# Other durations in a planner's model: scans, DMA packets and operations off partition 0, with all offsets derived anew

## The chip, the core and the metric

The kernel runs on one core of a Trainium2 chip. The metric is the device time of one execution in microseconds (us). The time shown for a kernel is the median of its runs; beside it stands one profiled execution with a time of its own, from which all durations below are read. The core's engines are PE (matmuls; PEld are its weight loads), DVE (vector), ACT (scalar), POOL and SP, which here issues nearly all DMAs. Each engine runs its instructions in the order in which they stand in its queue and waits at the first one that is not ready.

## The reference

Three parts in a row, for 4 batches, 8 heads, 768 steps, head size 40:

```python
for t in range(S):                      # attention: a recurrence over a 40x40 state per head
    y[:, :, t] = einsum('bhd,bhde->bhe', rt, state)
    Sa = einsum('bhde,bhe->bhd', state, at)
    state = state * wt - einsum('bhd,bhe->bhde', Sa, bt) + einsum('bhd,bhe->bhde', vt, kt)
x = y as [3072, 320]
h = x @ w_in;  x = (h * cos(h)) @ w_out                          # first MoE, 320 -> 2048 -> 320
h = x @ w_in2; out = (h * clip(h + 3, 0, 6) / 6) @ w_out2        # second MoE
```

## The kernel before, in words

The recurrence is cut into 12 chunks of 64 steps. Work is done per chunk c and batch b (unit n = 4c + b). Values are kept as pairs of fp16 numbers (a high and a low part), so a product is several matmuls.

Per unit, `pA`, `pB`, `pT`, `pC` load the inputs (raw), multiply them by decays (pip), make fp16 pairs (KBs, ARs), transpose them by DMA (KBT, ART) and form the triangular matrix (LN, NT), which `pL` stores. Per chunk, for all batches and heads at once, the inverse of that matrix is made: `iL` loads the triangles (Lt<-Ls), `iB` runs 31 steps on DVE, each a product into tmp and an addition into Tt, `iC` copies the result (four copies S8a<-Tt among them) and `iC1` sends it through DRAM (Tm<-Tt, Tm<-S8a, Thl<-Tt, then Lt<-Tm and TT<-Thl). `iD` and `iE` multiply 32x32 blocks on PE (tile q), and each of the two `iE` of a chunk ends with a DVE operation TT<-q,TT. Then come the units' recurrence steps `cV`, `cU`, `cA`, `cAT`, `cG`, `cF` (tiles FS, uh, GF, xy, S8a, ST), and `cXT` transposes a unit's output by DMA into x1T, the input of the first MoE.

`mA(m, c, j)` is a group of 16 matmuls of MoE m (into tile h), an ACT function (s<-h), a DVE product (s) and the fp16 pair ghl; `mB` multiplies ghl by wout (tile acc). m = 0 reads x1T, m = 1 reads x2T. Chunk c's `mA` can begin when the four units of chunk c have their x1T.

At the start the decays are computed by scans (`decay`, tensor_tensor_scan over 650 elements, 24 of them), and the weights are loaded and converted in passing (`ld_w`, `prep_w`).

The order of all this is made by the class `Plan` while the program is built. Every operation is recorded with a duration (`rec`). `order` plays the engines forward with these durations: at each moment an engine takes, of the operations that are ready, the one with the best priority. A priority is the length of the work that hangs on an operation, plus offsets in the table `TUNE`, one entry for each kind of step (an offset for all, two for the first two chunks, a release time, and one for each operation of the step). `AHEAD` and `MARGIN` say when an engine stays idle for a better operation that is about to be ready. Some operations may go to either of two engines: casts and copies to DVE or ACT, elementwise ones to DVE or POOL; the plan takes whichever comes free. `emit` (lines 415 and 419) then writes the instructions in that order, so nearly every instruction in the trace has line 419 (or 415, for a copy on ACT) and is told by its tiles.

Of the kernel before, what the change touches and what calls it, by code (L numbers as in the profile page):

```python
# [45 lines left out]


TUNE = {
    "decay_const": (406, -4, -216, 2, (69, -5)),
    "decay0": (0, 509, 274, 0, (1, 42, -5, -44, -13, -34, -127, -64, -11, 116, -48, -99, 17, -40, -43, 12, -192,  # L50
        -141, -67, -15, -3, 6, -4, 32, -39, -1, -6, -10, 7, 22, -66, -28, -2, -6, 10, -7, -48)),
    "consts": (97, -153, -168, 11, (-19, 91, 1, -32, -33, 38, 4, -23, 79, 145, -9, 10, -75, 14, 4, 6, 11, -12, -35)),
    "consts1": (-254, 100, 347, 0, (-14,)),
    "consts2": (60, 417, 197, 0, (-11, -4, -48)),
    "pA": (0, 51, -99, 0, (-1, 41)),
    "pB": (0, -16, -1, 39, (0, 0, -1, 0, 0, 0, 1)),
    "pT": (-1, 70, -30, 0, (2,)),
    "pC": (-20, -1, -45, 0, (0, 2, -8, 14)),
    "pL": (1, 5, 467, 0, (-1,)),
    "rest": (124, -153, -38, 17, (-10, -2)),  # L60
    "dsq0": (-68, 293, -36, 0, (18,)),
    "chunk_decay": (-5, 51, -56, 118, (-27, 37, 3, 51)),
# [11 lines left out]
    "cAT": (-74, 88, -241, 0, (-60,)),  # L74
    "cD": (-18, 7, -10, 82, (-13,)),
    "cG": (-2, -8, 9, 21, (-28, 0, -11, -7, 20, -2)),
    "cF": (-13, 1, 0, 173, (-19, 0, 0, 6, 4, 4, 6, 0, 0, -3)),
    "cXT": (-45, -151, 140, 0, (1,)),
    "cST": (5, -4, -19, 35, (2, 2, -5, -2)),
# [19 lines left out]
    "wcol": (-50, 302, -353, 190, (-20, -7, 0, -170, 60, -60, 105)),  # L99
    "flags": (153, -38, 4, 0, (-83, -72, 51, 21, 31, -14, 76, 60, 30, -72, 81, -15, -68, -54, -25, 111, -3, -24,  # L100
        -19, 131, -91, -99, 96, -71, 64, -111)),
}
HALVES = ((0, 0), (1, 0))
SHARE = 20
SLACK, AHEAD, MARGIN = [132, 0, 20, 0, 383], [0, 150, 70, 54], [422, 48, 296, 22]
RING = {"raw": 2560, "KBT": 2048, "LN": 2048, "v": 1280, "uh": 640, "FT": 2048, "gm": 2048, "pd": 2560, "xy": 1280,
        "wst": 2048, "wx": 1024, "s": 2048, "xs2": 1536, "ghl": 2048, "E": 1280, "ART": 2048, "NT": 1152}

# [25 lines left out]
T_SHAPE = 96.0  # L134
FULL = (128, 128)
POOL_GAIN = 0.25
LAT = {"PE": 190, "DVE": 125, "ACT": 140, "POOL": 70}


class Plan:  # L140
# [9 lines left out]
    def cover(self, ap):  # L150
        t = ap.tensor
        es = mybir.dt.size(ap.dtype)
        dims = [(a, b) for a, b in ap.ap if b > 1 and a]
        off = ap.offset
        dram = t._space == DRAM
        u = 32 if dram else 2
        key = (off, tuple(dims), es)
        m = self.masks.get((t.name, key))
        if m is not None:
            return m  # L160
        p0, p1 = 0, 1
        if not dram:
            row = 1
            for k in t.shape[1:]:
                row *= k
            p0, off = divmod(off, row)
            p1 = p0 + ap.ap[0][1]
            dims = [(a, b) for a, b in list(ap.ap)[1:] if b > 1 and a]
        off += sum(a * (b - 1) for a, b in dims if a < 0)
        dims = sorted((abs(a), b) for a, b in dims)  # L170
        run = 1
        while dims and dims[0][0] <= run:
            run += dims[0][0] * (dims[0][1] - 1)
            dims.pop(0)
        lo, hi = off * es // u, -(-(off + run) * es // u)
        if not dram:
            hi += sum(a * (b - 1) for a, b in dims) * es // u
            dims = []
        m = (1 << (hi - lo)) - 1
        for a, b in dims:  # L180
            sh, k = a * es // u, 1
            while 2 * k <= b:
                m |= m << sh * k
                k *= 2
            m |= m << sh * (b - k)
        m = (p0, p1, m << lo)
        self.masks[t.name, key] = m
        return m
# [20 lines left out]
    def rec(self, attr, eng, name, a, kw):  # L209
        i = len(self.ops)  # L210
# [9 lines left out]
        if name.startswith("dma"):  # L220
            sb = outs[0] if outs[0].tensor.__class__.__name__ == "Tile" and outs[0].tensor._space != DRAM else ins[0]
            c = 475.0 if sb.shape[0] in (32, 128) or ins[0].ap[0][0] == 0 else 650.0
            by = 1
            for k in outs[0].shape:
                by *= k
            by *= mybir.dt.size(outs[0].dtype)
            if name == "dma_start":
                run = _run(outs[0], ins[0])
                dma = by / 360.0 * (2 if run < 512 else 1)
            else:  # L230
                r, w = ins[0].shape[0], by // 2 // ins[0].shape[0]
                dma = w / 128 * 112 * r / 128
                c = 1244.0 if r == 128 and w >= 1024 else 1175.0
        elif eng == "PE":
            c = max(n / 2.4 + 2.5, 28.0)
            shape = tuple(32 if x <= 32 else 64 if x <= 64 else 128 for x in (ins[0].shape[0], _free(ins[0])))
        elif eng in ("DVE", "ANY"):
            c = 70 + n * 1.042
            es = max(mybir.dt.size(x.dtype) for x in outs + ins)
            if name == "tensor_copy":  # L240
                c = 70 + n * (0.26 if es == 2 else 0.52)
            elif name == "tensor_scalar":
                c = 70 + n * 0.52
            elif name == "reciprocal":
                c = 70 + n * 6.3
            if any(_free(x) == 1 for x in ins):
                c += 60
        elif eng == "ACT":
            c = 95 + n * 0.833
            if "accum_out" in kw:  # L250
                c += 93
            elif "bias" in kw:
                c += 50
            elif ins[0].tensor._space == PSUM:
                c -= 42
# [11 lines left out]
            o["shape"] = shape  # L267
        else:
            o = dict(eng=eng, c=c, alt=cp if eng in ALTS else None, dma=dma, deps=set(), prio=self.prio, calls=[],
                     grp=(self.group, outs[0].tensor.name), i=i, port=False, shape=FULL)  # L270
            self.ops.append(o)
            if eng == "PE" and shape != FULL:
                o["c"] += 2 * T_SHAPE
                o["shape"] = shape

            o["port"] = name not in ("memset", "tensor_reduce", "reciprocal") and all(getattr(x.tensor, "_space", None) != PSUM for x in ins)
        o["calls"].append((attr, name, a, kw))
        for x in ins:
# [4 lines left out]
    def order(self):  # L283
# [36 lines left out]
        soon = [set() for _ in engs]  # L320
        evs = []
        start = [0] * n
        gone = set()
        dmaf = dge = end = 0

# [36 lines left out]
        while evs:  # L362
# [14 lines left out]
            for e in sorted(touched):  # L377
# [7 lines left out]
                if e < 4 and AHEAD[e] > 0:  # L385
                    lim = 100 * t + c * AHEAD[e]
                    if any(100 * ready_t[u] < lim and pr[u] < pr[i] - 400 * MARGIN[e] for u in soon[e]):
                        continue
                gone.add(i)
                o["on"] = engs[e]  # L390
                start[i] = t
# [57 lines left out]
def _free(ap):  # L449
    n = 1  # L450
    for k in ap.shape[1:]:
        n *= k
    return n


def _run(o, i):
# [1012 lines left out]
```

## Time and profile before

| | us |
|---|---|
| median of 3 runs | 1272.9 |
| lowest, highest | 1268.25, 1284.62 |
| the profiled execution, its own time | 1271.3 |
| its span in the profile | 1269.4 |
| mean granted TensorE clock of the profiled execution | 0.935 of 2.4 GHz |

The span is from the first to the last instruction; 1.9 us of the execution's time lie around it. Rows of the trace name an engine, a line, an operation, its tiles as out<-in with partitions x elements, and times in us from the span's start. PEclk is the granted clock: 1.00 is 2.4 GHz, 0.50 is 1.2 GHz. "Idle before" is the time that an engine stood still ahead of an instruction, with the engine or DMA that ended it.

### The profile page before, as it was taken

The numbers are of one execution on the slowest core, as the hardware profiler recorded it, in microseconds if no ns is written. First come the engines' busy times: TensorE is split into PE (matmuls) and PEld (weight loads), VectorE is DVE, ScalarE is ACT, GpSimd is POOL, SyncE is SP. The second block draws the span as 40 slices with busy tenths as digits, with TensorE's granted clock in tenths as the row PEclk, the third lists the DMA queues.
The fourth block names the chain that finished last, engine by engine and source line by source line (L and its number), as shares of the span: only waits on it lengthen the run. The fifth ranks groups of instructions, "written<-read, shape, count | busy, mean of one in ns | idle before, by whom it ended". The sixth has DMA issues, their size and how long they took to land.

```text
span 1269.4 us, 29683 instructions
## 1 busy us (share of the span) xinstructions
PE 910.1 (72%) x11378; PEld 732.8 (58%) x11378; DVE 1067.0 (84%) x2434; ACT 792.8 (62%) x1642; POOL 180.4 (14%) x206
## 2 busy tenths in 40 slices
PE   0010033571668889699899898988999899999995
PEld 0000023561457668577777676766777777778874
DVE  8999999889989988869989799698796997967543
ACT  1664358485678667657676577686766866645352
POOL 2322111123423110101000010010120100100000
PEclk9999999795679899789999899899898999999998
DMA  6997478775787584776767748868477674532010
GB/s 204 244 186 177 107 225 151 159 162 124 149 171 148 108 156 102 134 144 103 130 143 135 142 83 151 148 113 155 103 126 150 115 134 93 94 63 46 11 24 14
DMA packets 474362, 162.65 MB, mean 128 GB/s; under 512 B 446789, under 2 KB 456049, under 8 KB 473826
## 3 DMA queue, kind: packets, MB, share of 16 engines
q1 hardware_dynamic: 473922, 160.00, 62.6%
q8 instruction: 91, 1.49, 0.5%
q10 hardware_dynamic: 288, 0.67, 0.2%
q14 instruction: 61, 0.50, 0.1%
HBM read 80.10 MB, written 25.61 MB: 83 GB/s over the span
## 4 chain that ended last, share of the span: by engine, by line
DVE 42%; PE 23%; DMA 11%; ACT 8%; issue 6%; SPq 3%; POOL 0%; DVEq 0%; ACTq 0%; POOLq 0%
PE acc L419 9%; PE h L419 8%; DVE Tt L419 6%; DVE tmp L419 5%; DVE S8a L419 4%; DVE ghl L419 4%; DVE wout L419 4%; PE q L419 4%; DVE s L419 3%; SPq L419 3%; DMA Lt<-Tm 2%; DVE win L419 2%; PE t L419 2%; DVE FS L419 2%; DVE GF L419 2%
## 5 line engine op out<-in xcount | busy, mean ns | idle before, releaser
L419 PE MATMUL acc<-wout,ghl 128*128 128x320 f16 x2304 | 371.8, 309 | 36.7 <-DVE ghl L419 29.6
L419 PEld LDWEIGHTS <-win 128*128 128x128 f16 x3328 | 312.1, 101 | 74.3 <-issue 27.6
L419 PEld LDWEIGHTS <-ghl 128*128 128x128 f16 x2304 | 217.1, 100 | 122.2 <-DVE ghl L419 35.1
L419 PE MATMUL h<-x1T,win 128*128 128x256 f16 (+1 forms) x1664 | 192.9, 275 | 25.4 <-DVE s L419 17.5
L419 ACT ACTIVATE s<-h,cvec 128x512 f32<-128x512 f32 x192 | 130.4, 680 | 119.4 <-PE h L419 81.8
L419 PE MATMUL h<-x2T,win 128*128 128x256 f16 (+1 forms) x1664 | 187.0, 267 | 0.0
L419 DVE TENSOR_TENSOR ghl<-s,ghl 128x512 f16<-128x512 f32 x182 | 127.6, 703 | 8.7 <-ACT ghl L415 5.2
L419 PE MATMUL p<-ART,KBT 120*128 120x64 f16 x384 | 21.4, 204 | 124.1 <-DMA ART<-ARs 73.7
L419 DVE TENSOR_TENSOR tmp<-Tt,Lt 128x126 f32<-128x126 f32 (+22 forms) x372 | 104.9, 282 | 6.5 <-DMA Lt<-Ls 3.3
L419 DVE TENSOR_TENSOR Tt<-Tt,tmp 128x126 f32<-128x126 f32 (+22 forms) x372 | 103.6, 279 | 3.6
L415 ACT ACTIVATE ghl<-s 128x512 f16<-128x512 f32 x127 | 79.3, 625 | 34.7 <-DVE s L419 27.3
L419 DVE SCALAR_TENSOR_TENSOR s<-h,s 128x512 f32<-128x512 f32 x96 | 65.7, 686 | 38.0 <-ACT s L419 37.5
L419 DVE SCALAR_TENSOR_TENSOR s<-s,h 128x512 f32<-128x512 f32 x96 | 65.2, 680 | 33.6 <-ACT s L419 33.2
L419 PEld LDWEIGHTS <-KBT 120*128 120x128 f16 x384 | 18.7, 104 | 127.7 <-DMA KBT<-KBs 84.7
L419 PE MATMUL t<-E,GF 128*128 128x40 f16 x1152 | 46.1, 184 | 40.1 <-DVE GF L419 32.3
L419 PE MATMUL q<-Lt,Tt 32*32 32x32 f32 x768 | 32.9, 203 | 49.3 <-DMA Lt<-Tm 49.3
L419 PEld LDWEIGHTS <-GF 128*128 128x128 f16 x1152 | 38.7, 99 | 49.1 <-DVE GF L419 34.5
L419 POOL TENSOR_TENSOR wout<-wout 128x512 int32<-128x512 int32 (+1 forms) x28 | 50.2, 1802 | 103.4 <-ACT wout L419 73.2
L419 PEld LDWEIGHTS q<-Lt,Tt 32*32 32x32 f32 x768 | 30.1, 118 | 53.5 <-issue 35.9
L419 PE MATMUL t<-FS,NT 128*128 128x40 f16 x768 | 36.7, 183 | 22.2 <-DVE FS L419 12.4
L419 POOL TENSOR_TENSOR S8a<-S8a,pd 40x320 f32<-40x320 f32 x23 | 25.7, 1123 | 176.0 <-DMA pd<-Ds 175.6
L419 PEld LDWEIGHTS <-ART 120*64 120x64 f16 (+1 forms) x704 | 43.9, 106 | 6.7 <-issue 4.4
(157 smaller groups left out, 1764.1 us busy)
## 6 DMA issues: line engine op xcount, KB each, us to landing
raw<-in_arbk_dram SPq DMA_DIRECT2D x46, 320.0 KB
v<-in_vv_dram SPq DMA_DIRECT2D x96, 80.0 KB
pip<-Dec SPq DMA_DIRECT2D x46, 160.0 KB
wout<-in_moe_w_in_dram SPq DMA_DIRECT2D x12, 512.0 KB
Ls<-LN SPq DMA_DIRECT2D x48, 128.0 KB
Lt<-Ls SPq DMA_DIRECT2D x48, 128.0 KB
TT<-Thl SPq DMA_DIRECT2D x12, 512.0 KB
wstat<-in_moe_w_out_dram SPq DMA_DIRECT2D x10, 512.0 KB
```

The lines of the kernel that those rows point to most:

```text
L415: self.nc.scalar.activation(func=AF.Copy, **kw)
L419: getattr(getattr(self.nc, attr), name)(*a, **kw)
```

## The change

Four durations in the planner's model change. A scan is booked at 70 + 2.08 n ns instead of 70 + 1.042 n. A DMA is booked by its packets, 9 ns and 0.045 ns a byte each over 16 engines, instead of 360 GB/s with a doubling under 512 bytes; a DMA transpose at 204 instead of 112 ns for 128 columns. An operation of DVE or ACT whose output or input starts off partition 0 takes 110 ns more, and so does the one behind it. The key under which the planner keeps an access also has its number of partitions. With that model all numbers of `TUNE`, `AHEAD` and `MARGIN` are derived anew.

```diff
 TUNE = {
-    "iL": (2, 22, -1287, 19, (-27, 0, -88, 35)),
+    "iL": (4, -6, -1396, 19, (-1, -36, -88, 10)),
...
-SLACK, AHEAD, MARGIN = [132, 0, 20, 0, 383], [0, 150, 70, 54], [422, 48, 296, 22]
+SLACK, AHEAD, MARGIN = [132, 0, 20, 0, 383], [0, 164, 69, 10], [319, 48, 324, 54]
...
+OFFSET = 110
...
-        key = (off, tuple(dims), es)
+        key = (off, tuple(dims), es, ap.ap[0][1])
...
                 run = _run(outs[0], ins[0])
-                dma = by / 360.0 * (2 if run < 512 else 1)
+                run = min(run, 20480)
+                dma = by / run * (9 + run * 0.045) / 16
             else:
                 r, w = ins[0].shape[0], by // 2 // ins[0].shape[0]
-                dma = w / 128 * 112 * r / 128
+                dma = w / 128 * 204 * r / 128
...
+            elif name == "tensor_tensor_scan":
+                c = 70 + n * 2.08
...
+            o["off"] = OFFSET if any(_part(x) for x in outs[:1] + ins) else 0
...
+        was = [0] * 5
...
+                if e in (1, 2):
+                    c, was[e] = c + max(o["off"], was[e]), o["off"]
...
+def _part(ap):
+
+    row = 1
+    for k in getattr(ap.tensor, "shape", ())[1:]:
+        row *= k
+    return ap.offset >= row
```

(Engine 1 is DVE, engine 2 is ACT.) What the program computes stays as it is, and each engine has as many instructions as before but for a few that change engines; their order is another nearly everywhere. Two places show it.

The first is DVE's queue in chunk 7, from the middle of the work behind the last inverse step up to the first TT<-q,TT. Before, 19 instructions stand between that step and this TT; these are the last of them:

```order
L419 SCALAR_TENSOR_TENSOR s_147<-h_145,s_147 128x512
L419 TENSOR_TENSOR ghl_150<-s_148,ghl_150 128x512
L419 TENSOR_TENSOR S8a<-S8a,pd_142 40x320
L419 TENSOR_TENSOR ghl_151<-s_147,ghl_151 128x512
L419 SCALAR_TENSOR_TENSOR s_148<-h_146,s_148 128x512
L419 CAST ghl_149<-s_148 128x512
L419 TENSOR_TENSOR ghl_149<-s_148,ghl_149 128x512
L419 SCALAR_TENSOR_TENSOR s_147<-h_145,s_147 128x512
L419 TENSOR_TENSOR LN_135<-p_134,mskL 128x512
L419 CAST NT_115<-LN_135 64x512
L419 TENSOR_TENSOR ghl_150<-s_147,ghl_150 128x512
L419 SCALAR_TENSOR_TENSOR TT<-q_137,TT 32x16x32
```

In the new order 26 instructions stand between the two, and these are the last:

```order
L428 TENSOR_TENSOR ghl_149<-s_148,ghl_149 128x512
L428 TENSOR_TENSOR NT_114<-LN_135,NT_114 64x512
L428 SCALAR_TENSOR_TENSOR s_147<-h_145,s_147 128x512
L428 CAST ghl_150<-s_147 128x512
L428 TENSOR_TENSOR ghl_150<-s_147,ghl_150 128x512
L428 SCALAR_TENSOR_TENSOR s_148<-h_146,s_148 128x512
L428 CAST ghl_151<-s_148 128x512
L428 TENSOR_TENSOR ghl_151<-s_148,ghl_151 128x512
L428 TENSOR_TENSOR raw_116<-raw_116,pip_80 128x640
L428 CAST KBs_76<-raw_116 128x8x2x40
L428 SCALAR_TENSOR_TENSOR TT<-q_137,TT 32x16x32
```

One more MoE group (s, ghl) and a unit's raw and KBs operations, which stood behind the TT, now stand ahead of it.

The second is SP's queue in the same chunk, from the first store of the inverse to the load that brings it back (Lt<-Tm). Before:

```order
L419 DMA Tm_106<-Tt 64x16x32
L419 DMA Tm_106<-S8a 64x16x32
L419 DMA Thl_108<-Tt 64x16x32 x4
L419 DMA_TRANSPOSE KBT_125<-KBs_77 128x8x128
L419 DMA Lt_92<-Tm_106 64x1024
L419 DMA Ls_103<-LN_135 64x16x32
```

After:

```order
L428 DMA Tm_106<-Tt 64x16x32
L428 DMA Srep_89<-Tt 40x16x40
L428 DMA Thl_108<-Tt 64x16x32
L428 DMA Tm_106<-S8a 64x16x32
L428 DMA Thl_108<-Tt 64x16x32 x3
L428 DMA_TRANSPOSE ART_129<-ARs_79 128x8x128
L428 DMA Ls_103<-LN_135 64x16x32
L428 DMA Lt_92<-Tm_106 64x1024
```

The load keeps its place behind the stores; a store of LN, an ART transpose and one of the three Srep copies have come in front of it, and a KBT transpose has gone elsewhere.

## Rows read from the trace of the kernel before

**Rows 1.** The page, busy us (share of the span) and instructions of each engine.

```profile
PE 910.1 (72%) x11378; PEld 732.8 (58%) x11378; DVE 1067.0 (84%) x2434; ACT 792.8 (62%) x1642; POOL 180.4 (14%) x206
```

**Rows 2.** The chain that ended last, share of the span by engine.

```profile
DVE 42%; PE 23%; DMA 11%; ACT 8%; issue 6%; SPq 3%; POOL 0%; DVEq 0%; ACTq 0%; POOLq 0%
```

**Rows 3.** Busy time by stage: stretch, its length, each engine's busy us, granted clock.

```profile
core 0: us, PE busy (x) PEld busy (x) DVE busy (x) ACT busy (x) POOL busy (x), PEclk, DMA share, GB/s
...
534.00:1163.00 629.00, 576.21 (x7242) 462.28 (x7239) 531.84 (x1294) 425.86 (x921) 53.99 (x77) 0.96 0.65 120
1163.00:1247.00 84.00, 84.00 (x726) 67.00 (x724) 41.86 (x86) 34.92 (x72) 0.00 (x0) 1.00 0.10 19
```

**Rows 4.** The same table for the round trips: chunk 7, and the sum over ten.

```profile
786.90:813.10 26.20, 22.22 (x261) 16.84 (x261) 15.28 (x26) 14.79 (x30) 2.25 (x6) 0.87 0.91 145
...
sum 261.50, PE 227.33 PEld 178.16 DVE 171.65 ACT 152.25 POOL 24.74; mean PE 22.73 PEld 17.82 DVE 17.16 ACT 15.22 POOL 2.47
```

**Rows 5.** The same table for the nine stretches between the round trips, summed.

```profile
sum 515.30, PE 460.85 PEld 372.65 DVE 494.59 ACT 382.17 POOL 62.06; mean PE 51.21 PEld 41.41 DVE 54.95 ACT 42.46 POOL 6.90
```

**Rows 6.** The chain of work within 785 to 815 us: start, us, what.

```profile
795.73 3.75 DMA Lt<-Tm
799.52 1.19 PE q L419 x32
...
802.11 1.84 PE q L419 x32
...
804.86 3.41 PE h L419 x16
...
812.99 1.76 PE h L419 x16
```

**Rows 7.** DVE's timeline there; in brackets the idle time before and its end.

```profile
804.61 0.69 DVE L419 SCALAR_TENSOR_TENSOR TT<-q,TT 32x512 f16<-32x512 f32 x1 [1.65 <-ACT TT L419]
...
809.03 0.69 DVE L419 SCALAR_TENSOR_TENSOR s<-h,s 128x512 f32<-128x512 f32 x1 [3.02 <-ACT s L419]
```

**Rows 8.** The table by stretch, for the clock in chunks 7 and 3.

```profile
795.00:801.50 6.50, 4.65 (x68) 3.79 (x67) 3.26 (x6) 1.41 (x3) 0.00 (x0) 1.00 1.04 200
801.50:808.30 6.80, 6.80 (x57) 4.60 (x56) 2.77 (x5) 1.55 (x3) 0.00 (x0) 0.50 0.90 131
...
521.00:528.30 7.30, 2.73 (x63) 2.24 (x62) 6.42 (x18) 4.47 (x10) 1.47 (x1) 0.73 0.54 117
```

**Rows 9.** Groups by form: count, busy us, mean ns of one, idle before.

```profile
L419 DVE TENSOR_TENSOR_SCAN win<-win 128x650 f32<-128x650 f32 x24 | 38.2, 1607 | 3.7 <-DMA win<-in_wfwd_dram 3.3 <-ACT win L419 0.3
...
L419 DVE CAST ghl<-s 128x512 f16<-128x512 f32 x65 | 28.4, 437 | 10.0 <-PE acc L419 8.0
```

**Rows 10.** DVE's timeline at 608 to 611 us: start, us, instruction.

```profile
608.14 0.69 DVE L419 TENSOR_TENSOR LN<-p,mskL 128x512 f32<-128x512 f32 x1
608.74 0.27 DVE L419 TENSOR_TENSOR tmp<-Tt,Lt 128x120 f32<-128x120 f32 x1
...
609.82 0.69 DVE L419 TENSOR_TENSOR NT<-LN,NT 64x512 f16<-64x512 f32 x1
610.53 0.29 DVE L419 TENSOR_TENSOR tmp<-Tt,Lt 128x121 f32<-128x121 f32 x1
```

**Rows 11.** PE's timeline at the end of chunks 3 and 10.

```profile
522.13 0.57 PE L419 MATMUL t<-E,GF 128*128 128x40 f16 x16
...
1094.70 5.05 PE L419 MATMUL acc<-wout,ghl 128*128 128x320 f16 x36
```

**Rows 12.** The chain of work within 522 to 529 us.

```profile
525.77 2.47 DMA x1T<-S8a
```

**Rows 13.** PE's waits, 534 to 1131 us: us in total, times, longest.

```profile
PE q L419 <- DMA Lt<-Tm: 12.2, 7, 2.6
...
PE h L419 <- DMA x1T<-S8a: 3.3, 4, 1.1
```

More of the change, by code (lines that the diff above doesn't have):

```diff
@@ L48 @@
 TUNE = {
[L49 to L62, printed above, removed]
[11 rows of a table removed]
[L74 to L77, printed above, removed]
@@ L78 @@
-    "cXT": (-45, -151, 140, 0, (1,)),
-    "cST": (5, -4, -19, 35, (2, 2, -5, -2)),
[19 rows of a table removed]
-    "wcol": (-50, 302, -353, 190, (-20, -7, 0, -170, 60, -60, 105)),
-    "flags": (153, -38, 4, 0, (-83, -72, 51, 21, 31, -14, 76, 60, 30, -72, 81, -15, -68, -54, -25, 111, -3, -24,
-        -19, 131, -91, -99, 96, -71, 64, -111)),
+    "decay_const": (245, -5, -183, 3, (81, -521)),
+    "decay0": (-412, 438, -1354, 0, (1, 86, -5, -22, -13, -34, -127, -66, -9, 120, -85, -107, 6, -42, -25, -4,
+        -198, -188, -70, -16, -3, 6, -4, 63, -39, -1, -4, -16, 7, 14, -122, -28, -17, -7, -37, 95, 40)),
@@ new lines @@
+    "consts": (23, 47, -328, 13, (-16, 139, 7, -139, -49, 9, 4, -32, 215, 155, -173, 91, -79, 14, -4, 8, 11,
+        -19, -132)),
+    "consts1": (-322, 100, 347, 14, (174,)),
+    "consts2": (72, 409, 113, 0, (-15, 19, -44, -81, 0, -19, 9, 49, -18)),
+    "pA": (-4, -195, -99, 14, (4, 39)),
+    "pB": (0, -35, -1, 30, (8, 0, -1, 0, 0, 0, 1)),
+    "pT": (-9, 69, -55, 0, (102, -1)),
+    "pC": (-20, -1, -45, 0, (0, 2, 1, 38)),
+    "pL": (3, 5, 958, 0, (6,)),
+    "rest": (132, -153, 95, 5, (-31, -57)),
@@ new lines @@
+    "dsq0": (-56, 21, -34, 4, (29,)),
+    "chunk_decay": (-23, 55, 173, 120, (26, 28, -2, 73)),
[11 rows of a table added]
+    "cAT": (-96, 88, -328, 0, (-165,)),
+    "cD": (-14, -55, 0, 60, (-16, 3)),
+    "cG": (-2, -8, 9, 26, (-28, 0, -11, -8, 23, -2)),
+    "cF": (-13, 1, 0, 178, (-30, 0, -220, 6, 4, 4, 6, 0, 0, -4)),
+    "cXT": (-156, -151, -324, 0, (88,)),
+    "cST": (15, -4, 123, 58, (2, 16, -5, -2)),
[19 rows of a table added]
+    "wcol": (-127, 264, -374, 242, (-44, 12, 0, -167, 179, 13, 105)),
+    "flags": (291, -252, -106, 0, (-79, -95, 51, 24, 83, 290, 150, -33, 30, 46, 81, 57, -70, -52, -26, 69, -205,
+        -40, -82, 111, -105, -151, -49, -154, -39, 48)),
@@ L269, in rec @@
             o = dict(eng=eng, c=c, alt=cp if eng in ALTS else None, dma=dma, deps=set(), prio=self.prio, calls=[],
-                     grp=(self.group, outs[0].tensor.name), i=i, port=False, shape=FULL)
+                     grp=(self.group, outs[0].tensor.name), i=i, port=False, shape=FULL, off=0)
             self.ops.append(o)
```

56 rows, old and new, of the table TUNE are left out of this document.

## The prediction

> **What bounds the kernel now.** I read the page's busy shares first. DVE is busy for 84% of the span and PE for 72% [rows 1], so no engine is full on average, and the chain that ended last goes through DVE for 42%, PE for 23% and DMA for 11% [rows 2]. An average over stages hides the limits, so the table by stage comes next [rows 3]. From 534 to 1163 us DVE works 532 of 629 us and PE 576: both are near 90%, and neither reaches it alone. From 1163 to 1247 us PE is busy throughout: this is what is left of the MoE once the last attention chunk is through.
>
> Then I cut the middle by what the program does. Once per chunk DVE finishes 31 inverse steps (iB); the triangle goes out to DRAM and back (Tm stores, Lt load), PE multiplies it (iD, iE) and DVE folds the result into TT. I call the stretch from the last inverse step to the second such TT a round trip. The ten round trips of chunks 2 to 11 last 261.5 us, in which DVE works 171.7: 90 us idle [rows 4]. The nine stretches between them last 515.3 us with DVE at 494.6: 21 us idle [rows 5]. So four fifths of DVE's idle time lies in a third of the time. PE is the mirror image: it idles 34 us in the round trips and 54 us between them. Each engine waits where the other one limits; a gain must even out the two.
>
> Chunk 7 shows why. The Lt load is issued at 795.73 and takes 3.75 us, PE stands at iD until 799.52, and the group of 16 h matmuls behind it takes 3.41 us, where the same group takes 1.76 us at 812.99 [rows 6]. DVE meanwhile stands at TT for 1.65 us and at an s for 3.02 us [rows 7]. The granted clock is 1.00 (2.4 GHz) up to 801.5, with PE busy 4.65 of 6.5 us, and 0.50 (1.2 GHz) in the 6.8 us after it [rows 8].
>
> **The change, part by part.** The planner only decides where instructions stand; it issues no new work. Two of its new durations are right by the trace. A scan takes 1607 ns [rows 9]; the old rule books 70 + 650 x 1.042 = 747 ns, the new one 1422. An operation off partition 0 is not overlapped with its neighbours: LN starts at 608.14, lasts 0.69 and its successor starts after 0.60, while NT<-LN (it reads LN from partition 64) starts at 609.82, lasts 0.69 and its successor starts after 0.71 [rows 10]. That is 0.11 us on either side, the planner's 110 ns. So the old plan handed DVE less time than it takes, and everything timed against DVE came out wrong by that. What the new order does with this I take in four terms.
>
> Term A, where copies run. The order moves 14 casts of ghl (437 ns each [rows 9]) and 14 copies of GF onto DVE, and takes 16 casts of xy, 8 copies of pip and some fifteen half-tile operations off it. Summing over every DVE instruction ahead of the last chunk's last xy the mean duration of its form, I get 1045 us in the old order and 1040 in the new one: -5 us. ACT takes 26 more off-partition instructions that stand alone; at 0.11 us on either side that is under 6 us on an engine that is busy for 62% [rows 1]. I cost it at nothing, since DVE's and PE's own work lies beside it; without that cover it would cost those 6 us.
>
> Term B, the cover of the round trips. DVE's instructions between the last inverse step and the second TT add up to 171.7 us over chunks 2 to 11 in the old order (what the trace shows as busy) and, by the same mean durations, to 203.2 us in the new one. That is 31.5 us of work moved from the stretches where DVE limits into those where it waits. Chunk 7 goes from 15.7 to 20.4 us. Its upper bound is all 31.5 us. Its lower bound is 0: the work is there, but PE feeds it, and PE works 22.7 of 26.2 us in a round trip already. I counted PE's matmul work between the last s whose input DVE has used and iD, less DVE's work in that time: over chunks 3 to 11 it averages 13.2 us in the old order (9.3 to 18.3) and 14.1 in the new one (12.5 to 15.3). So PE's lead grows by 0.9 us per chunk, 8 us over nine, and it is even. Between 8 and 31.5 I take 18: most of the idle time before TT is covered by DVE's own work (raw, KBs and NT operations that need no PE), but each s still waits for PE. On SP the load stands behind three Thl stores and one Ls or ART, as before, so I expect it no earlier.
>
> The row above on the clock bears on this. By the Trainium skill, TensorE: Matmul & The Clock Gate, section on Part 1, the throttled state is the default and activity releases it, so a PE that no longer stands at iD would keep 2.4 GHz. The trace agrees in the order of events: the half clock came right after the wait. By the rule the whole of term B is to be had, -31.5 us; by PE's lead alone it is -8.
>
> Term C, the hand-over to the MoE. The first matmul of chunk c's MoE needs the last x1T transpose of its attention. Where PE had nothing to put between, in chunk 3, its last attention matmul ended at 522.7 [rows 11] and the transpose landed at 528.2 [rows 12]: 5.5 us. The old order has 6.1 to 8.0 us of PE work in that gap in chunks 4 to 10, the new one 3.9 to 4.7 (36 acc matmuls are 5.05 us [rows 11]). So PE will wait 0.8 to 1.6 us in seven chunks, where it now waits 3.3 us in all [rows 13]: 8 less 3, +5 us. Behind the waiting matmul PE's queue holds acc matmuls whose ghl is ready, and DVE waits for the s that follow; with a slower x1T, as ACT now makes the cast, +2.4 each or +17. From -3 (no wait at all) to +17 I take +5.
>
> Term D, the tail. Behind the last attention matmul the old order keeps 400 h and 342 acc matmuls, the new one 384 and 339. 16 h are 1.76 us [rows 6] and three acc 0.4: -2 us. PE is full there [rows 3], so this counts in full.
>
> Sum: -5 - 18 + 5 - 2 = -20 us. The profiled execution took 1271.3 us around its span of 1269.4; that gives 1251. The median of the runs shown, 1272.9, is 1.6 higher, so 1253; an order is only as good as its weakest wait, and I keep 2 us of that for stalls that I don't see, which makes 1255.
>
> **Rivals.**
> 1. Full cover: PE no longer stands at Lt and keeps 2.4 GHz. For it: its waits there are 12.2 us in seven times [rows 13], and in chunk 7 the group at half clock cost 3.41 - 1.76 = 1.65 us more and DVE 3.02. Against it: PE's lead hardly grows. Price: -5 - 31.5 - 2 + 1.6 on 1271.3 = 1234 us.
> 2. The change does not do what it says: the idle time moves out of the round trips into the stretches between them, since the work moved into the one is missing in the other, and there PE's 54 us of idle grow. For it: each stretch loses some 3.5 us of DVE work, PE was waiting for DVE there, and the first s of a chunk comes with x1T. Then only A and D are left: 1266 us.
> 3. Slower: the wait for x1T decides. From the point where PE stands there long enough for its clock to fall, each of seven chunks pays the wait of up to 2.4 us and half of a stretch of 6.8 us at 1.2 GHz, 3.4 us, while DVE gets no s: 7 x 5.8 = 41 us, against -5 - 8 - 2. For it: chunk 3, where PE was busy 2.73 of 7.3 us and the granted clock was 0.73 [rows 8]. Against it: PE's waits for x1T are at most 1.1 us in chunks 4 to 11 [rows 13]. It gives 1271.3 + 26 + 1.6 = 1299 us.
>
> **How the numbers follow.** The forecast, 1255 us, has a chance of 0.50, rival 1 0.20, rival 2 0.20, rival 3 0.10. Terms B and C alone let the forecast run from 1240 to 1268. The range, 1234 to 1281, takes in the first rival's time and the second's and leaves out the worse part of the third. A measurement of this kernel can tell about 2%: below 1247.4 or above 1298.4 us. Below lie the first rival and a fifth of the forecast, 0.30; above, half of the third rival and a little for what I don't see, 0.07; within, 0.63.
>
> **What would show it.** Right: DVE's busy share in the round trips rises from 66% towards 75%, its waits at s and TT there halve, and the last xy comes near 1145 us instead of 1163. Term C shows as PE waiting for x1T some 8 us in all. If PE's wait for Lt and the clock of 0.50 behind it are gone, rival 1 holds; if the stretches between the round trips show more DVE idle than 21 us, rival 2; if the half clock follows x1T, rival 3. I am wrong in kind if the last xy comes no earlier, or if the time is lost before 354 us, where I moved nothing.

## The result and the profile after

| | before | after |
|---|---|---|
| median, us | 1274.65 (4 runs) | 1233.07 (4 runs) |
| lowest, highest | 1268.25, 1284.62 | 1232.29, 1233.55 |
| ratio, 95% interval | | 0.9714 [0.9679, 0.9748] |
| span of the profiled execution | 1269.4 | 1231.3 |

The ratio compares fast runs alone, here and below, so it is not always the quotient of the medians. The change makes the kernel 2.9% faster. The median is 22 us under the forecast of 1255 and 1 us under the range of 1234 to 1281; the ratio on the 1272.9 us that the forecast started from gives 1236.5. The page's row of busy times and the table by stage of the new kernel (columns as in [rows 1] and [rows 3]; the two stages run from the last inverse step of chunk 4 to the last xy, and from there to where PE's MoE work ends):

```profile
PE 900.5 (73%) x11378; PEld 727.2 (59%) x11378; DVE 1055.4 (86%) x2430; ACT 795.2 (65%) x1645; POOL 194.2 (16%) x207
```

```profile
523.40:1128.00 604.60, 560.90 (x7193) 453.27 (x7192) 523.38 (x1293) 421.89 (x911) 53.57 (x79) 0.98 0.68 124
1128.00:1209.00 81.00, 81.00 (x699) 64.48 (x698) 42.16 (x86) 32.31 (x69) 0.00 (x0) 1.00 0.10 20
```

The middle stage took 629.0 us [rows 3] and takes 604.6; the tail is full of PE work as before and 3 us shorter. The same cut as in [rows 4, 5]: chunk 7's round trip and the sum over ten, then the sum over the nine stretches between:

```profile
761.40:787.80 26.40, 25.84 (x324) 20.93 (x323) 19.94 (x37) 17.60 (x35) 3.83 (x8) 1.00 0.83 141
...
sum 252.50, PE 243.07 PEld 194.51 DVE 201.44 ACT 171.42 POOL 30.57; mean PE 24.31 PEld 19.45 DVE 20.14 ACT 17.14 POOL 3.06
```

```profile
sum 501.90, PE 440.85 PEld 356.16 DVE 461.56 ACT 365.17 POOL 60.81; mean PE 48.98 PEld 39.57 DVE 51.28 ACT 40.57 POOL 6.76
```

DVE idles 252.5 - 201.4 = 51.1 us in the round trips, where it idled 89.9 [rows 4], and 40.3 us between them, where it idled 20.7 [rows 5]. So 38.8 us of idle time went out of the one and 19.6 came into the other: half is given back. The load Lt<-Tm is not what comes earlier: over chunks 2 to 11 it is issued 8.2 us behind the last inverse step on average, 7.9 before. PE's waits in the same part, against [rows 13]:

```profile
PE h L428 <- DMA x1T<-S8a: 19.6, 7, 4.1
PE t L428 <- DVE GF L428: 3.5, 4, 1.7
PE q L428 <- DMA Lt<-Tm: 3.3, 5, 1.3
```

The wait for Lt is nearly gone (12.2 before), the wait for x1T has grown from 3.3 to 19.6, and the half clock has moved with it. The chain of work in chunk 6 and the table by stretch there show it:

```profile
746.92 2.96 DMA x1T<-S8a
749.88 0.04 issue
749.92 3.44 PE h L428 x16
```

```profile
743.00:749.70 6.70, 2.79 (x46) 2.07 (x44) 6.50 (x22) 4.49 (x12) 0.00 (x0) 1.00 0.77 142
749.70:753.10 3.40, 3.17 (x16) 2.18 (x16) 1.94 (x6) 1.20 (x2) 0.00 (x0) 0.50 0.84 161
```

PE is busy for 2.79 of 6.7 us, waits for the transpose, and the 16 h matmuls behind it take 3.44 us at a granted clock of 0.50 (1.76 at full clock [rows 6]).

The surprise lies at the start. Up to the last xy of chunk 2 the kernels compare so (same columns; first the whole stretch, then the part from chunk 1's second TT to chunk 2's last inverse step). Before:

```profile
0.00:425.60 425.60, 149.64 (x2222) 123.82 (x2223) 392.42 (x796) 257.58 (x498) 117.53 (x117) 0.89 0.73 167
...
253.30:354.50 101.20, 53.65 (x671) 42.31 (x668) 91.56 (x203) 70.37 (x144) 34.52 (x21) 0.73 0.69 155
```

After:

```profile
0.00:410.30 410.30, 152.71 (x2273) 126.52 (x2274) 385.30 (x789) 262.23 (x507) 129.69 (x114) 0.93 0.75 172
...
252.60:340.90 88.30, 43.20 (x557) 33.76 (x555) 82.61 (x191) 62.08 (x128) 35.92 (x20) 0.71 0.65 151
```

15.3 us are gained here, 12.9 of them in the one part (which also has 9 us less DVE work in it), on a DVE that is busy for 92% of the whole stretch in the old kernel and 94% in the new one. A sum over DVE's records up to a chunk's last xy puts the whole gain in its place. Occupied is the time in which at least one operation runs, small gaps are those under 0.16 us, idle is the rest:

| DVE up to the last xy of | time | occupied | small gaps | idle |
|---|---|---|---|---|
| chunk 2, before / after | 425.6 / 410.3 | 393.0 / 385.8 | 5.1 / 4.5 | 27.3 / 19.7 |
| chunk 11, before / after | 1162.6 / 1127.9 | 1020.5 / 1008.7 | 21.3 / 22.6 | 120.6 / 96.3 |

Of the span's 38.1 us, 15.3 are gained by chunk 2 (7.2 occupied, 7.6 idle), 19.4 from there to the last xy (4.6 occupied, 16.7 idle, gaps +1.9), and 3.4 in the tail.

### The profile page after: what moved, and what is told of

Same layout as the page of the kernel before. It is cut to its first block, busy times and chain, and to the rows that moved or that the text cites. A ratio compares the mean times of both kernels' runs of the same rounds, so it can differ in the third digit from the quotient of the medians.

```text
span 1231.3 us, 29701 instructions
## 1 busy us (share of the span) xinstructions
PE 900.5 (73%) x11378; PEld 727.2 (59%) x11378; DVE 1055.4 (86%) x2430; ACT 795.2 (65%) x1645; POOL 194.2 (16%) x207
## 5 line engine op out<-in xcount | busy, mean ns | idle before, releaser
L428 PE MATMUL acc<-wout,ghl 128*128 128x320 f16 x2304 | 363.9, 304 | 15.8 <-DVE ghl L428 15.3
L428 PE MATMUL h<-x1T,win 128*128 128x256 f16 (+1 forms) x1664 | 198.3, 279 | 29.8 <-DMA x1T<-S8a 22.2
L428 PE MATMUL h<-x2T,win 128*128 128x256 f16 (+1 forms) x1664 | 183.9, 266 | 3.0 <-DVE s L428 3.0
L428 DVE TENSOR_TENSOR ghl<-s,ghl 128x512 f16<-128x512 f32 x178 | 122.1, 689 | 5.0 <-ACT ghl L424 0.6
L428 PE MATMUL p<-ART,KBT 120*128 120x64 f16 x384 | 21.3, 203 | 120.2 <-DMA ART<-ARs 64.4
L428 DVE TENSOR_TENSOR tmp<-Tt,Lt 128x126 f32<-128x126 f32 (+22 forms) x372 | 101.0, 272 | 4.6 <-DMA Lt<-Ls 1.6
L428 PEld LDWEIGHTS <-KBT 120*128 120x128 f16 x384 | 17.9, 104 | 124.9 <-DMA KBT<-KBs 92.5
L424 ACT ACTIVATE ghl<-s 128x512 f16<-128x512 f32 x113 | 70.2, 623 | 20.9 <-DVE s L428 16.9
L428 POOL TENSOR_TENSOR wout<-wout 128x512 int32<-128x512 int32 (+2 forms) x29 | 57.6, 1994 | 90.1 <-ACT wout L428 56.2
L428 PEld LDWEIGHTS <-GF 128*128 128x128 f16 x1152 | 38.7, 99 | 46.3 <-DVE GF L428 23.6
L428 ACT ACTIVATE FS<-v 128x640 f16<-128x640 f32 x48 | 35.1, 731 | 20.2 <-DMA v<-in_vv_dram 12.5
```

The source lines that it names most:

```text
L424: self.nc.scalar.activation(func=AF.Copy, **kw)
L428: getattr(getattr(self.nc, attr), name)(*a, **kw)
```

## The experiments

All times are medians; ratios are against the kernel before, run on the same chip (1275.5, 1271.3 and 1271.6 us in the three sets). The rows and sums are from one profiled execution of each. Theory 1 is: DVE's and PE's work now lies in the round trips, and that is the gain. Its rivals are PE's clock and the new order as one whole.

**Is it the wait for Lt?** In the old order I put iD and iE later:

```diff
+            if g[0] in ("iD", "iE") and g[2] > 1:
+                key[i] += 3400          # ns of planned time, old order
```

> The kernel before, with one thing moved in its order: the iD and iE of chunks 2 to 11 (PE, ACT and DVE parts) stand 3.4 us of planned time later, so that one more MoE group lies between the inverse and iD. Theory 1 (the round trip is what costs, and cover for it is what the change gave): PE's wait for Lt<-Tm falls from 14.5 us to under 5, the half clock right behind iD goes, DVE's idle time in the ten round trips falls from 90 us to 60 to 70, and the time falls by 12 to 25 us, to 1248 to 1261. Rival 1 (the gain belongs to the whole order, a single place moves its wait on): the wait turns up at the next step that needs TT, and the time stays within 6 us of the kernel before.

Measured 1298.5 us, 1.0228 [1.0148, 1.0309]. PE no longer waits for Lt, and the kernel is slower. The sum over its ten round trips, and the first rows of PE's waits from 530 to 1130 us:

```profile
sum 311.20, PE 262.98 PEld 203.13 DVE 203.68 ACT 175.89 POOL 26.98; mean PE 26.30 PEld 20.31 DVE 20.37 ACT 17.59 POOL 2.70
```

```profile
PE h L420 <- DVE s L420: 15.9, 14, 2.4
PE t L420 <- ACT TT L420: 9.2, 4, 3.5
PE q L420 <- ACT S8a L420: 8.6, 9, 2.6
```

The round trips are 50 us longer. PE's work stands ahead of iD as wanted, but TT comes later and PE then waits for TT and for the copy between iD and iE. DVE has 203.7 us of work in them, as much as in the new order, and gains nothing by it: it idles 107.5 us there. Work in the round trip is a cover only if the round trip isn't lengthened for it. My expectation fell; the rival had the moved wait right, and not the time.

**Is it PE's stock ahead of iD?** In the new order I put the MoE matmuls of the last 3.6 us ahead of each iD behind it:

```diff
+            if o["eng"] == "PE" and g[0] in ("mA", "mB"):
+                for c in range(2, NC):
+                    if lead[c] - 3600 <= key[i] < lead[c]:   # lead[c]: planned start of chunk c's iD
+                        key[i] = lead[c] + 1
```

> The changed kernel, with the MoE matmuls of the last 3.6 us of planned time before each iD of chunks 2 to 11 put behind it. Theory 1: PE stands at iD again for 2 to 3 us in each chunk, 20 to 30 us in all, the clock falls to 1.2 GHz behind it, and the time rises by 10 to 25 us over the changed kernel, to 1243 to 1258. Rival 1: the order absorbs it, within 6 us of 1233.

Measured 1285.9 us, 1.0131 [1.0055, 1.0207]: 53 us above the new kernel, more than expected. The profiled execution took 1293.6 us, the longest of the four. PE's first row of waits (530 to 1130 us), the sum over the round trips, and PE's timeline in chunk 7 from the first iD to the first iE, in this run and then in the new kernel:

```profile
PE q L429 <- DMA Lt<-Tm: 21.3, 7, 4.5
```

```profile
sum 312.00, PE 270.58 PEld 209.82 DVE 201.37 ACT 172.36 POOL 29.87; mean PE 27.06 PEld 20.98 DVE 20.14 ACT 17.24 POOL 2.99
```

```profile
803.93 1.67 PE L429 MATMUL q<-Lt,Tt 32*32 32x32 f32 x32 [3.36 <-DMA Lt<-Tm]
805.54 3.38 PE L429 MATMUL acc<-wout,ghl 128*128 128x320 f16 x12
808.71 3.10 PE L429 MATMUL h<-x1T,win 128*128 128x256 f16 x16
811.65 1.39 PE L429 MATMUL acc<-wout,ghl 128*128 128x320 f16 x9
813.20 1.19 PE L429 MATMUL q<-Lt,S8a 32*32 32x32 f32 x32 [0.17 <-ACT S8a L429]
```

```profile
774.83 1.19 PE L428 MATMUL q<-Lt,Tt 32*32 32x32 f32 x32 [0.53 <-DMA Lt<-Tm]
775.96 1.40 PE L428 MATMUL acc<-wout,ghl 128*128 128x320 f16 x9
777.28 1.19 PE L428 MATMUL q<-Lt,S8a 32*32 32x32 f32 x32
```

The wait for Lt is back, the round trips are 60 us longer with the same DVE work in them, and DVE's idle time there is 110.6 us in place of 51.1. But the edit did two things. The moved matmuls no longer stand ahead of iD, and they now stand between iD and iE: 7.7 us of matmuls there in chunk 7, where the new kernel has 1.3. Over chunks 2 to 11 the first iD begins as early as in the new kernel (12.6 and 12.9 us behind the last inverse step), and the first TT begins 6.0 us later (23.6 and 17.6), which is the whole 60 us. So the run shows what matmuls between iD and iE cost. What the stock ahead of iD is worth it doesn't show.

**Is it the clock?** Matmuls that only keep PE busy, ahead of the wait, tell the clock from the wait. In the old order at Lt, in the new one at x1T:

```diff
+        if o["eng"] == "PE" and g[0] == "iD" and g[2] > 1 and g[3] == 0:            # old order
+            for _ in range(16):
+                self.nc.tensor.matmul(self.fq[g[2]][:, 0:256], self.fill[:, 0:128], self.fill, start=True, stop=True)
+        if o["eng"] == "PE" and g[0] == "mA" and g[2] == 0 and g[3] > 1 and g[4] == 0:   # new order
+            hp, w = o["calls"][0][2][:2]
+            for _ in range(20):
+                self.nc.tensor.matmul(hp, w, self.fill, start=True, stop=True)
```

> The old order, and ahead of the first iD of chunks 2 to 11 16 matmuls of 256 columns that read only the weights and write the q tile which iD then overwrites (1.76 us at 2.4 GHz; PE's waits for Lt there are 12.2 us in seven times). Theory 1: DVE's idle time in the round trips is for want of its own work and for TT, not for PE's clock; DVE idle stays near 90 us in the ten round trips and the time within 6 us of the old kernel's. Rival, the clock: the 0.50 behind iD goes away in six chunks, 1.65 us per h group and up to 3 us of DVE's wait for an s each: 15 to 25 us faster than the old kernel, about half of what the new order gained.

Measured 1264.5 us, 0.9947 [0.9917, 0.9978], 6.8 us faster than the old kernel. Chunk 7 in that run, PE's timeline with the filler (L416) and the first iD, DVE's timeline at the first TT and the s behind it, and the table by stretch:

```profile
796.14 1.91 PE L416 MATMUL q<-win 128*128 128x256 f16 x16
798.05 1.19 PE L423 MATMUL q<-Lt,Tt 32*32 32x32 f32 x32
```

```profile
802.18 0.69 DVE L423 SCALAR_TENSOR_TENSOR TT<-q,TT 32x512 f16<-32x512 f32 x1 [0.69 <-ACT TT L423]
...
804.77 0.69 DVE L423 SCALAR_TENSOR_TENSOR s<-h,s 128x512 f32<-128x512 f32 x1 [1.18 <-ACT s L423]
```

```profile
798.00:805.00 7.00, 7.00 (x135) 5.89 (x135) 3.41 (x6) 3.22 (x6) 0.00 (x0) 1.00 0.94 192
...
sum 254.30, PE 232.66 PEld 187.55 DVE 170.36 ACT 152.05 POOL 24.31; mean PE 23.27 PEld 18.76 DVE 17.04 ACT 15.20 POOL 2.43
```

The clock stays at 1.00 behind iD, DVE's wait for that s is 1.18 us in place of 3.02 [rows 7], and yet its idle time in the ten round trips is 83.9 us in place of 89.9: its waits for s there fell from 31.3 to 19.9 us, and its waits for DMAs rose from 15 to 22. Between 530 us and the last xy the half clock falls from 47.6 to 13.6 us. So the clock at Lt is real and worth 7 us, a sixth of the gain, with the filler's own cost to PE taken off.

> The new order, and ahead of each chunk's first h group (chunks 2 to 11) 20 matmuls of 256 columns that read only the weights and write the h tile which the group behind them then overwrites. They last about 2.1 us at 2.4 GHz (16 such take 1.76 us) and fill most of PE's nine waits for x1T (22.2 us in all, up to 4.1). Theory 1 (what the new order gained is work for DVE during the round trips; PE's clock behind its own waits costs little): the wait shrinks by what the filler takes, the first s of the chunk comes no earlier, 1228 to 1240 us. Rival, the clock: in the new order the granted clock is 0.50 for 3.4 to 10.2 us behind eight of these waits, so PE loses some 3 us per chunk there; with the filler the clock stays at 1.00 and the time falls by 10 to 25, to 1208 to 1223 us.

Measured 1236.1 us, 0.9696 [0.9639, 0.9753]: the same as the new kernel. The wait is 6.5 us in place of 19.6 and the clock is 1.00 throughout chunk 6's hand-over:

```profile
PE h L433 <- DMA x1T<-S8a: 6.5, 6, 1.5
```

```profile
746.00:756.00 10.00, 7.17 (x90) 6.19 (x87) 7.82 (x24) 6.34 (x15) 0.00 (x0) 1.00 0.84 168
```

The half clock behind x1T, which the new kernel has in six chunks (4 to 9, not in eight, as I had written), is gone in all of them (10 us of it turn up at two other places), and the time is not better. The filler itself takes 2.35 us, and summed over the chunks whose wait was shorter that is 6 us more work for PE; within the intervals, some 7 us to either side, the clock's price in the new order is about that or less. In the stretches between the round trips DVE is busy for 92%, and they last 503.0 us with the filler and 501.9 without. The profiled execution is the longest of the four, 1240.9 us. The filler takes the half clock away, and it does not bring x1T or the first h any earlier.

**Can the wait for x1T be planned away?**

```diff
+            if g[0] == "mA" and g[2] == 0 and g[3] > 1 and g[4] == 0:
+                key[i] += 2500          # the first h group of a chunk, new order
```

> The changed kernel, with the first MoE group of each chunk from 2 on 2.5 us of planned time later, so that other PE work lies before the wait for x1T. Theory 2 (the new wait for x1T, 22 us, and the half clock right behind it are on the path and give back part of the gain): the wait falls under 10 us, the half clock behind it goes, and the time falls by 5 to 12 us, to 1221 to 1228. Rival 2 (DVE is behind there, and PE's wait is hidden): within 4 us of 1233, though the wait falls.

Measured 1251.0 us, 0.9875 [0.980, 0.995], 18 above the new kernel, and the wait is still there (first two rows of PE's waits, 530 to 1130 us):

```profile
PE h L429 <- DMA x1T<-S8a: 19.7, 7, 4.1
PE h L429 <- DVE s L429: 11.3, 12, 1.7
```

PE got other waits, for s, in addition. As a test of what the wait for x1T is worth this run is inconclusive, since it didn't take it away.

**Two gains or one?** The order written out, one kernel's up to the last xy of chunk 2 and the other's from there:

```diff
+seq = new[:k + 1] + [i for i in old if i not in new[:k + 1]]     # k: last xy of chunk 2; the counterpart with new and old exchanged
```

> The order written out: as in the new kernel up to the last xy of chunk 2, from there the rest as in the old one, engines of the movable operations included. In the new kernel the last xy of chunk 2 comes 15 us earlier than in the old one, and the other 19 of the 35 us by the last xy of chunk 11 are gained behind it. Theory 1 (two separate gains, one in the first stage and one in the round trips): the early 15 us stay, 1253 to 1263 us, with the old waits of PE for Lt and DVE idle near 90 us in the round trips. Rival (an order is one whole, and its parts don't add): the mixed order loses the early gain again in the chunks behind, 1268 us or more.

Measured 1258.0 us, 0.9888 [0.9828, 0.9949].

> The counterpart: the old order up to the last xy of chunk 2, from there the rest as in the new kernel. Theory 1: only the gain of the round trips, 19 to 23 us, is there: 1247 to 1256 us, DVE idle in the round trips of chunks 3 to 11 near 47 us in place of 85. Rival (parts don't add): 1265 us or more.

Measured 1255.0 us, 0.9863 [0.9805, 0.9921]. Both times are as theory 1 had them; DVE's idle time in chunks 3 to 11 of the second is 54 us, not 47. With the new start, chunk 2's last xy comes at 410.8 and the rest goes at the old pace: 738.2 us to the last xy of chunk 11, 737.0 in the old kernel. With the old start it comes at 424.0 and the rest takes 725.4, against 717.6 in the new kernel. Against the old kernel's median the two gains are 13.3 and 16.3 us, 30 of the 38 between 1271.3 and the new kernel's 1233.1; the rest goes where the two orders join, or behind. The sums over the ten round trips, of the first kernel and of the second, show which has the cover:

```profile
sum 263.70, PE 236.47 PEld 185.24 DVE 177.70 ACT 158.30 POOL 26.71; mean PE 23.65 PEld 18.52 DVE 17.77 ACT 15.83 POOL 2.67
```

```profile
sum 253.90, PE 236.42 PEld 189.13 DVE 194.59 ACT 165.23 POOL 28.81; mean PE 23.64 PEld 18.91 DVE 19.46 ACT 16.52 POOL 2.88
```

DVE idles 86.0 us in the one (old: 89.9) and 59.3 in the other (new: 51.1).

**Order or engines?** The order and the engine of the 352 movable operations that differ, exchanged one at a time:

```diff
+seq, on = old_order, new_engines      # and: seq, on = new_order, old_engines
```

> The old order written out, but each of the 352 movable operations whose engine differs in the new kernel (124 from DVE to ACT, 121 back, 54 from DVE to POOL, 53 back) runs on the engine that it has there. Theory 1 (term A is a gain by itself: DVE's work ahead of the last xy falls by 12 us in the new kernel because fewer operations off partition 0 and half tiles stand on DVE): 1261 to 1268 us, 5 to 12 below the old kernel. Rival (engines and order belong together: an operation put on an engine that is not free there makes those behind it wait): 1280 us or more.

Measured 1279.7 us, 1.0075 [1.004, 1.0109].

> The counterpart: the new order written out, each movable operation on the engine that it has in the old kernel. Theory 1 (the order carries the gain of the round trips, the engines some 12 us of DVE's work): 1240 to 1250 us. Rival (engines and order belong together): 1260 us or more, with DVE idle in the round trips well above 51 us.

Measured 1256.5 us, 0.9892 [0.9859, 0.9925]. By the last xy of chunk 11 DVE's records give:

| order | engines | median, us | profiled execution, us | DVE occupied | DVE idle |
|---|---|---|---|---|---|
| old | old | 1271.6 | 1271.3 | 1020.5 | 120.6 |
| old | new | 1279.7 | 1272.5 | 1023.4 | 120.9 |
| new | old | 1256.5 | 1253.2 | 1023.8 | 100.0 |
| new | new | 1233.1 | 1233.4 | 1008.7 | 96.3 |

The order alone takes 20.6 us of idle time from DVE. The new engines take 15 us of occupied time from it, but only in the order that was made with them. In the old order DVE's records show no gain, and the median is 8 us higher; where these 8 us lie the records can't show, since the profiled execution is the fastest of its ten. (That of the new order with the old engines is the fastest of ten as well, 3 us under the median.) Neither theory holds as written: the order has a gain of its own, and the engines have one only together with it.

**Model or offsets?** The new durations with the old TUNE, AHEAD and MARGIN, then the counterpart, then the new kernel with one duration set back:

```diff
-SLACK, AHEAD, MARGIN = [132, 0, 20, 0, 383], [0, 164, 69, 10], [319, 48, 324, 54]
+SLACK, AHEAD, MARGIN = [132, 0, 20, 0, 383], [0, 150, 70, 54], [422, 48, 296, 22]    # first kernel; and TUNE
-                c = 70 + n * 2.08
+                c = 70 + n * 1.042                                                    # third kernel
```

> The new durations with the old offsets (TUNE, AHEAD and MARGIN of before). Theory 3 (the durations give the gain, the offsets only polish it): 1235 to 1250 us. Rival 3 (the offsets found for the durations give it; old offsets in a new model are out of place): 1265 us or more.

Measured 1285.1 us, 1.0127 [1.005, 1.0204]: right durations with offsets made for the wrong ones are slower than before, as rival 3 had it.

> The new TUNE, AHEAD and MARGIN, planned with the old four durations. The new durations with the old offsets gave 1.0127 of the old kernel's time. Theory 1 (the offsets are good only with the durations for which they were derived): 1275 us or more, 1.00 to 1.03. Rival (the offsets carry the gain by themselves, the durations add nothing): 1230 to 1250 us.

Measured 1272.7 us, 1.0007 [0.9967, 1.0047]: no difference to before, in theory 1's range by the ratio; the rival falls.

> The new kernel with one duration set back: a scan is booked at 747 ns in place of 1422 (the trace has 1607). All 24 scans lie in the first stage. Theory 1 (this duration is what evens the first stage, the rest of the order stays good): the 15 us by the last xy of chunk 2 are lost and the later 19 to 23 kept, 1244 to 1254 us. Rival (the offsets fit one model only, a single duration set back reorders all that follows and costs as much as the whole old model): 1260 us or more, with DVE idle in the round trips of chunks 3 to 11 well above 48 us.

Measured 1268.0 us, 0.9971 [0.9932, 1.001]: the rival holds. The last xy of chunk 2 comes at 420.7, so 10 of the early 15 us are lost, but the later gain goes too: DVE's idle time in the round trips is 77.4 us (283.6 less 206.2; 51.1 in the new kernel), with more DVE work in them than the new kernel has. A duration for 24 scans in the first stage reorders the kernel to its end. The model alone costs 1.3%, the offsets alone give nothing, and both together give 2.9%.

## Why the prediction was right and wrong

**What was right.** The work that the new order puts into the round trips: 203.2 us forecast, 201.4 measured (DVE's busy share there is 80%, past the 75 that I wrote). That DVE's waits at s and TT there would halve: 31.3 and 24.1 us before, 12.8 and 16.0 after. That the load comes no earlier, though in chunk 7 the queue ahead of it is not "as before" (four Thl stores and a KBT in the old one, three Thl, an ART and an Ls in the new one). That the last xy would decide and the tail give a little: -2 forecast, -3.4 measured.

**Where the missing time is.** My terms had 20 us of the span's 38. Of the 18 that they lack, 6.8 are occupied time of DVE (term A, -5 against -11.8), 7.6 are idle time in the first stage, for which I had no term, 3.7 are idle time behind chunk 2 (B and C, -13 against -16.7), 1.4 lie in the tail, and small gaps take 1.3 back. The forecast is off by 22 because I added 2 us for stalls and 1.6 for the median. That B and C together came out near the measured sum is luck, as the next two parts show. By their own bounds (B from -31.5 to -8, C from -3 to +17) these two let the forecast run from 1233.5 to 1277 us, further than the 1240 to 1268 that I gave.

**Term B was too small.** I let 18 of 31.5 us count, because PE's lead grew by only 0.9 us a chunk and "each s still waits for PE". Measured are 38.8 us of idle time, above my upper bound, in round trips that became 9 us shorter. The step that failed is the lead as one sum of matmul work. PE's idle time in the round trips fell from 34.2 to 9.4 us, and DVE's waits for s there from 31.3 to 12.8, with a lead of nearly the same size. The DVE work alone doesn't make the gain: e6 and e5 have as much of it (203.7 and 206.2 us), in round trips of 311 and 284 us, and the one is slower than the old kernel, the other no different from it. In the new order the first TT comes as early as in the old one (17.6 and 17.9 us behind the last inverse step). That a more even lead of PE is what allows this is my reading; no run shows it.

**Term C was too small as well**, and hid this. I forecast 5 us, with 8 of waits for x1T. The waits are 19.6 us, and DVE idles 19.6 us more between the round trips (the same number by chance). The step that failed is the 5.5 us from the last attention matmul to the first h, which I took from one chunk of the old kernel. In chunks 4 to 10 of the new one they are 4.9 to 8.4 us, 7.2 on average, with 3.5 to 4.3 us of PE work between. The old trace could have told: in its chunks 4 to 10 the last transpose of a chunk is issued 2.0 to 7.2 us behind the last attention matmul, in chunk 3 it is 3.1. DVE's idle time lies there: in the 6 us behind the first h matmul of the nine hand-overs in these stretches it idles 16.0 us in the new kernel and 1.9 in the old one. Chunk 6, behind the h at 749.92:

```profile
754.17 0.69 DVE L428 SCALAR_TENSOR_TENSOR s<-h,s 128x512 f32<-128x512 f32 x1 [1.67 <-ACT s L428]
```

That is rival 2's event, and it took back half of term B: -38.8 + 19.6 = -19.2. My -18 + 5 = -13 was two misses that partly cancel. Whether the late x1T makes this idle time, or the 33 us of DVE work that have gone from these stretches into the round trips and would have filled it, isn't shown. The filler can't tell them apart: x1T lands no earlier with it, and DVE idles 14.0 us in these places and 41.4 us in all the stretches.

**Term A was too small.** I forecast -5 us from mean durations of forms, and had them right: with each operation's shortest duration the new engines take some 5 us from DVE. But DVE's occupied time fell by 11.8 up to the last xy, 7.2 of it by chunk 2. Some 7 us more are operations that last longer beside POOL (a sum over all DVE instructions that overlap a POOL instruction, of their duration less the shortest of the same instruction in six profiles: about 70 us before, 63 after). In this stretch of the new kernel's timeline the same kind of operation takes 0.42 us alone and 1.51 beside POOL:

```profile
145.97 0.42 DVE L428 TENSOR_SCALAR wstat<-wstat 128x512 int32<-128x512 int32 x1
...
147.38 1.53 POOL L428 TENSOR_TENSOR wstat<-wstat 128x512 int32<-128x512 int32 x1 [8.63 <-ACT wstat L428]
...
147.69 1.51 DVE L428 TENSOR_SCALAR wout<-wout 128x512 int32<-128x512 int32 x1
```

It ends 0.29 us after POOL's does. By the Trainium skill, SBUF — State Buffer, the section "SBUF: two separate sides", DVE, in a mode that uses two ports or with two SBUF inputs, and GpSimd share a port pair as an exclusive lock, and the second to start blocks until the first is done (with two SBUF inputs only against a GpSimd operation that reads SBUF); these rows agree with that, though none shows the mode in which this operation ran. A mean duration of a form averages over this and can't see that an order avoids it.

**The step that failed in kind is the first stage.** I wrote that I moved nothing ahead of 354 us, and DVE's idle time there had no term. 15.3 us are gained up to 425 us, and e11 shows that they stand by themselves (13.3 us). The diff changes the offsets of decay and prep_w too, and DVE is busy for 92% of that stretch: 7 us less occupied time and 7.6 less idle make up the gain. In e5 the duration of the scans, set back alone, loses 10 of the 15 us. I cut the middle into round trips and never made the same sum for the start.

**Rival 1 has the time, 1234 us, by luck.** Its events came: PE's wait for Lt is 3.3 us in place of 12.2, the half clock behind it is gone from chunk 3 on, and the cover is more than its 31.5 us. But it had nothing for the 19.6 us that came back between the round trips, and nothing for the first stage, and these two nearly cancel. Nor is the clock what makes the cover: e10 prices it at 7 us in the old order. On the clock its rule (the Trainium skill, TensorE: Matmul & The Clock Gate, Part 1: activity releases the throttled state) agrees with the runs: with the filler the granted clock stays at 1.00 at both places. What it would be worth does not follow from that.

**Rival 3 has the event and not the price.** Half clock follows x1T in six chunks, and the kernel is faster all the same. e9 takes it away, and nothing is left of a gain once the filler is paid.

Open stay: which of the many moves in the first stage make its 15 us; what the durations of DMAs and of operations off partition 0 do singly, since only that of the scans was set back alone; what PE's stock ahead of iD and the wait for x1T are worth, since the runs that changed them also put other PE work in the way; and why the exchanged engines lose overlap between neighbouring DVE operations (durations less occupied time are 133 and 132 us in the two kernels and 127 and 125 in the two exchanged ones), which is about half of the 15 us.

## What to carry to other kernels

Make the sum of a reordering for every stage, the first too, and for both sides of a move: idle time that goes out of one stretch can come back in the next, here by half. To find where an order gains, join it with the old one at a point in time, and exchange order and engines separately. Shifts of a single step by hand in a plan this tight cost 18 to 53 us whichever way they went, and a moved step lands on something: look where, before the time is read as the price of the place that it left. A planner's durations and its offsets belong together: the new offsets alone gave nothing, the new durations alone cost 1.3%.

## What the runs showed of the hardware

Taking a half clock away gave back less than half of the PE time that it took, once the filler is paid. In the old order there was 34 us less of it with the filler, and 16 h matmuls take 3.41 us at 0.50 and 1.76 at 1.00, so PE saves some 17 us by an estimate from these rows; the kernel gained 6.8. Filler matmuls (16 of 256 columns in 1.91 us, 20 in 2.35) kept the granted clock at 1.00 over a wait at both places; in the new order, where DVE is busy for 92% of the stretches around it, they gained nothing beyond their own cost. The other surprise is the size of POOL's effect on DVE: some 63 us of DVE's durations in the new kernel are added beside POOL instructions, and an operation of 0.42 us can take 1.51.
